# Attention and feed-forward in one hand-scheduled kernel: the adds of two vector engines kept apart in the built order, a cap on one engine's exps, and a reordered start

## The chip, the cores and the metric

The kernel runs on one core of a Trainium2 chip. The core has a matrix engine (TensorE, "PE" in the profile, with "PEld" for its weight loads), a vector engine (VectorE, "DVE"), a scalar engine (ScalarE, "ACT"), GpSimd ("POOL"), and a queue engine that issues DMAs (SyncE, "SP"). The engines run their own instruction lists and wait for one another by semaphores. The metric is the device time of one execution in microseconds; less is better.

## The reference

One token sequence (2048 x 640) is normalised and fed to two branches, whose results are added to the input.

```python
xn = _layernorm(x)                       # no scale, no bias
# A: attention, 32 query heads of 20, one shared key and value head
q = (xn @ wq) as [1, 32, 2048, 20];  k = xn @ wk;  v = xn @ wv
p = softmax(q k^T * 20 ** -0.5)
A = (p v, heads side by side) @ wo
# B: dense feed-forward of width 1728
B = silu(xn @ w1) @ w2
return x + A + B
```

Inputs and output are bfloat16.

## The kernel before

**How the work is tiled.** Scores are made transposed: a block is 128 keys of one head by 512 queries. There are 4 chunks of 512 queries, and in each 8 groups of 4 heads: 32 groups. A group has 16 key tiles (kt) times 4 heads (j) = 64 blocks, in the order kt, then j. Three blocks in a row are one step: `do_S` issues three score matmuls at once (each head lies in its own 32 rows), so there are 683 steps. Their three PSUM banks alternate between two sets of three.

**Two ways to make exp.** ScalarE turns two blocks of a step into exp with one ACTIVATE of 1024 columns (L841), or three with one of 1536. The third block usually goes to VectorE. `want_dve` decides: not in the first 8 steps, not in the last, not for the last two blocks of a group, and only if VectorE's planned backlog is under a threshold. VectorE's exp is an approximation by bits: L856 clips the score to a 16-bit integer (Z), which read as bfloat16 is a rough exponential. Two shifted copies of Z (Y) make it finer: the block's contribution is the sum of Z, Z+43 and Z+86, each multiplied with its own scaled copy of v. So a VectorE block gives three PV items and a ScalarE block one.

**The shifted adds.** `flush_z` collects up to three Z blocks and makes their two Y tiles: the second always on GpSimd (L888, int32 on pairs), the first on VectorE (L882) or GpSimd, by planned backlog.

**PV.** A round of `do_pv` takes up to one item from each of the four heads and multiplies them side by side in the four column strips of the array (L762). All rounds of a group add into one PSUM bank, U. When a group's items are done, VectorE copies U out (L931), a DMA transposes it, GpSimd divides (L920), and only then may the next group's rounds start. A head with more items than the others makes rounds in which fewer than four strips work. Exps of ScalarE wait for their round in a ring of 31 blocks (E).

**The rest of TensorE's work** is put in between the steps: query projections (`qd_job`, L977, spread to the heads by DMA), the hidden layer of the feed-forward (`h_job`, L1013, with a tanh on ScalarE at L1026 and a product on VectorE at L1031), and output rows (`out_job`, L1081 and L1086). `fill_chunk` gives each such job an earliest step, spread by PACE over the chunk. Where TensorE would stand idle and has recently been little used, `fill` adds matmuls on zeros (L684, L671), which keep its clock up.

**The order.** Nothing of the order is written out. `Sched` is a list scheduler that runs in Python when the kernel is built. Every operation has a planned duration and a priority (a smaller number first); each engine takes the ready operation with the least. TensorE's choice is `step`: S as soon as its banks are free, else a PV round or a job if it ends early enough before the next S is due (S_LEAD, OVER), else a fill. The lists are then fixed, and only true data dependences become semaphore waits. So planned times shape the order, but they do not hold an engine back on the chip.

**The lock.** `Op.lock` is part of that planning. An operation with the flag may not start, in planned time, before the last flagged operation of the other of VectorE and GpSimd has ended:

```python
if op.lock:
    r = max(r, self.lock_end["pool" if op.eng == "dve" else "dve"])
```

The VectorE adds carry it, and so do the norms, the division and the copies of k on GpSimd. GpSimd's adds (yp) do not.

**The prologue.** The input is loaded in 16 tiles, its statistics are taken on VectorE and ScalarE, the tiles are normalised on three engines and transposed, four to six on TensorE (L1453) and ten by DMA (L1421). `self.pro` is a queue of TensorE jobs, taken strictly from its head: four transposes, the first query tile (q0), k0, k1 and then the jobs of PRO. q0 and q1 (L952) give the queries of heads 0 to 3 and 4 to 7, each k job keys for two key tiles, each v job values for four. q1 needs its weights copied by ScalarE (L1316, priority 6; exps have 5). Step 21 is the first that reads q1. The zeros that the fills multiply are set by GpSimd (L1281).

Of the kernel before, what the change touches and what calls it, by code (L numbers as in the profile page):

```python
# [48 lines left out]
LATE_G = 0  # L49
AHEAD = 30  # L50
Q_FROM = 8
H0_STEP = 14
Y_SLOW = 0.1
H_FIRST = 4
NEARLY = 2
LASTPV = 16
DVE_LAST = 1
ZWAIT = 6
SWITCH = 0.105
S_LEAD = 0.56  # L60
PV_PRESS = 8
DVE_TH = 3.4
U_PRIO = 1.1
X_PRIO = 0.8
PACE = (0.9, 0.9, 0.9, 0.9)
WIN = 3.4
FILL_BELOW = 0.78
FILL_EARLY = 0.95
FILL_STEPS = 64
OVER = 0.1  # L70
PV_HOLD = 29
Q_EVERY = 2
DT_ISSUE = 1.28
UT_ISSUE = 1.05
DT = (4, 5, 6, 9, 10, 11, 12, 13, 14, 15)
NORM_P = 4.5
DVE_FROM = 8
NODB = 2
GB = 4 * KT
NB = NUNITS * KT  # L80
Y0_POOL = 1.0
Y0_COST = 1.45
YP_FIX = 0.14
YP_BLK = 0.47
PV_MIN = 4
PV_GO = 5
PRO = "v0 t7 t8 v1 k2 k3 k4 k5 v2 k6 k7 v3 q1 d0"
ACT_STATS = (4, 6, 9, 12, 14)
NW_ENG = ("dve", "dve", "dve")
NORM_ENG = ("pool", "pool", "pool", "pool", "act", "pool", "act", "act", "dve", "act", "act", "act")  # L90
# [254 lines left out]


def t_mm(n):
    return max(n, 64) / 2400.0 + 0.003


class Job:
# [15 lines left out]
class Builder:  # L367
# [88 lines left out]
    def steps_init(self):  # L456
        self.NG = NUNITS // 4
        self.T = -(-NB // 3)
        self.s_next = 0
        self.misc = deque()  # L460
        self.pro = deque()
        self.urgent = deque()
        self.cur_job = None
        self.pe_mode = None
        self.blk_pos = 0
        self.zset = 0
        self.zblocks = []
        self.exp_op = {}
        self.dve_steps = 0
        self.y0_pool = 0  # L470
        self.started = False
        self.pv_started = False
        self.tq = [[[] for _ in range(4)] for _ in range(self.NG)]
        self.begun = [False] * 4
        self.cg = 0
        self.g_seen = [0] * self.NG
        self.g_late = [0] * self.NG
        self.e_used = 0
        self.u_open = False
        self.u_last = []  # L480
        self.nfill = 0
        self.nqd = 0
        self.heldb = {}
        self.y_done = {}
        self.f_done = defaultdict(int)
        self.oT_made = set()
        self.pro_left = True
        self.filled = set()
        self.norm_made = defaultdict(int)
        self.first_step = {c: c * GB * 8 // 3 for c in range(QC)}  # L490
        self.first_step[QC] = self.T
# [80 lines left out]
    def step(self, now):  # L572
        sc = self.sc
        t = self.s_next
        sr = INF
        if t < self.T:
            sr = self.s_ready(t)
            if sr <= now + 1e-9:
                self.do_S(t, now)
                return True  # L580
        limit = INF
        if sr < INF:
            limit = sr
            e1 = self.exp_op.get(t - 1)
            if e1 is not None:
                endp = e1.end if e1.end is not None else sc.t["act"] + e1.dur
                limit = max(sr, endp - S_LEAD)
        pv_n, pv_some, pv_r = self.pv_ready(now)
        job = self.cur_job
        cand = None  # L590
        job_r = INF
        if job is None:
            for q in (self.urgent, self.pro, self.misc):
                if q:
                    r = self.job_ready(q[0])
                    if r <= now + 1e-9:
                        cand = q
                        break
                    job_r = min(job_r, r)
        has_misc = job is not None or cand is not None  # L600
        press = self.e_used > NBLK - PV_PRESS
        choice = None
        if pv_n and (self.pe_mode == "PV" or press):
            choice = "PV"
        elif has_misc and self.pe_mode == "M":
            choice = "M"
        elif pv_n >= PV_GO:
            choice = "PV"
        elif has_misc:
            choice = "M"  # L610
        elif pv_n:
            choice = "PV"
        nxt = min(sr, pv_r, job_r)
        if choice is None and pv_some >= (1 if press else PV_MIN):
            choice = "PV"
        if self.s_next >= self.T - LASTPV and (pv_n or self.s_next >= self.T and pv_some):
            choice = "PV"
        if choice is None:
            return self.fill(now, min(nxt, limit)) or nxt
        if choice == "PV":  # L620
            d = 0.216 + self.switch("PV")
        else:
            d = (job if job is not None else cand[0]).mms[0][0] + self.switch("M")
        if sr < INF and now + d > limit + OVER:
            return self.fill(now, limit) or (nxt if nxt > now else sr)
        if choice == "PV":
            self.do_pv(now, d)
        else:
            if job is None:
                job = cand.popleft()  # L630
                job.bank = self.bank_for_job(job)[1]
                self.cur_job = job
                if job.hold is not None:
                    self.heldb[job.hold] = job.bank
            self.do_mm(job, now, d)
        return True
# [10 lines left out]
    def fill(self, now, until):  # L647
        if self.s_next >= self.T and self.cg >= self.NG:
            return None
        sc = self.sc  # L650
        job = self.cur_job
        onto = job is not None and job.begun and job.width > 0 and (self.pe_mode == "M" or not self.u_open)
        mode = "PV" if self.u_open and not onto else "M"
        room = min(until, now + 0.33) - now - self.switch(mode)
        if room < 0.08 or self.busy_share(now) > (FILL_BELOW if self.s_next > FILL_STEPS else FILL_EARLY):
            return None
        n = min(512, int(room * 2400) // 32 * 32)
        after = ()
        if onto:
            n = min(n, job.width)  # L660
            b = job.bank
            ukey = ("B", b)

            def fn(pe):
                return pe.matmul(self.bk(b, 0, n), self.zero[:, 0:P], self.zero[:, 0:n], start=False, stop=False,
                                 skip_group_check=True)
        elif self.u_open:
            ukey = None

            def fn(pe):  # L670
                return pe.matmul(self.bk(UBANK, 0, n, 0, 32), self.zero[:, 0:32], self.zero[:, 0:n], start=False,  # L671
                                 stop=False, tile_position=(0, 0), skip_group_check=True)
        else:
            r, b = self.bank_for_job()
            ukey = ("B", b)
            if self.cur_job is not None or r > now + 1e-9:
                if not self.pv_started or self.u_open or not self.u_last:
                    return None
                if any(d.avail is None or d.avail > now for d in self.u_last):
                    return None  # L680
                b, ukey, after = UBANK, None, self.u_last

            def fn(pe):
                return pe.matmul(self.bk(b, 0, n), self.zero[:, 0:P], self.zero[:, 0:n], start=True, stop=True)  # L684
        z = sc.lastw.get(("zero",))
        if z is None or z.avail is None or z.avail > now:
            return None
        op = sc.new("pe", n / 2400.0 + self.switch(mode), fn, [("zero",)], [ukey] if ukey else [],
                    name="fill", queue=False)
        op.work = n / 2400.0  # L690
        op.deps.update(after)
        self.nfill += 1
        self.pe_mode = mode
        sc.commit(op, now)
        return True
# [51 lines left out]
    def do_pv(self, now, d):  # L747
# [24 lines left out]
            op.deps.add(sc.lastw[("vv", it.kt // 2)])  # L772
            self.e_used -= it.na
        op.mm = len(items)
        op.work = 0.216
        self.pe_mode = "PV"
        sc.commit(op, now)
        for it in items:
# [15 lines left out]

    def want_dve(self, t):
        g, kt, j = self.blocks(t)[-1]
        if t < DVE_FROM or 4 * kt + j >= GB - NODB or t >= self.T - DVE_LAST:
            return False
        sc = self.sc
        back = sc.t["dve"] - sc.t["pe"]  # L800
# [5 lines left out]
    def do_S(self, t, now):  # L806
# [42 lines left out]
        if dv:  # L849
            self.dve_steps += 1  # L850
            g, kt, j = bs[-1]
            zs, zp = self.zset, len(self.zblocks)
            bb = par3 + nh - 1

# [12 lines left out]
    def flush_z(self):  # L867
# [11 lines left out]
        for k, e in ((0, y0), (1, "pool")):  # L879
            yk = [("Y", zs, k, i) for i in range(n)]  # L880
            if e == "dve":
# [5 lines left out]
            cb = bass.AP(self.cy, c.offset, [list(c.ap[0]), [0, w // 2]])  # L887
            sc.new("pool", tp, lambda v, k=k, cb=cb: v.tensor_tensor(  # L888
                self.Y[:, zs, k, 0:w].bitcast(I32), self.Z[:, zs, 0:w].bitcast(I32), cb, ALU.add), zk + [("cy",)], yk,
                prio=4.0, name=f"yp{k}")  # L890
        for i, (t, g, kt, j) in enumerate(self.zblocks):
            for k in range(2):
                self.item(g, j, kt, k + 1, lambda k=k, i=i: self.Y[:, zs, k, i * QW:(i + 1) * QW].bitcast(BF16),
# [327 lines left out]
    def prologue(self):  # L1221
# [52 lines left out]
        def pool(d, fn, r, w, prio=0.0):  # L1274
            return np_("pool", d, fn, r, w, prio=prio, name="pool")
# [2 lines left out]
                                            fill=1.0, base=0, pattern=[[-1, P]], channel_multiplier=1),  # L1278
             [("idf",)], [("idf",)])
        pool(0.2, lambda g: g.tensor_copy(self.idb[:, :], self.idf[:, :]), [("idf",)], [("idb",)])  # L1280
        pool(0.3, lambda g: g.memset(self.zero[:, :], 0.0), [], [("zero",)])  # L1281
        pool(0.1, lambda g: g.memset(self.eps[:, :], EPS), [], [("eps",)])
        for k in range(2):
            pool(0.1, lambda g, k=k: g.memset(self.cy[:, k:k + 1], PH[k + 1][0] * 65537), [], [("cy",)])
# [300 lines left out]
```

## Time and profile before

| what | value |
|---|---|
| median of 3 runs | 739.06 us (738.40 to 739.63) |
| the profiled execution | 740.91 us, of which its instructions span 738.9 |
| mean granted clock of TensorE | 0.992 |
| first and last exp of ScalarE | start at 18.0 and 719.6 us |
| 60 to 719 us, busy of 659 | PE 639.4, DVE 609.4, ACT 644.0, POOL 461.3 |
| 719 to 738.9 us, busy of 19.9 | PE 16.5, DVE 8.3, ACT 3.2, POOL 2.5 |
| clock of TensorE at half | 0 to 7.2, 34.5 to 41.3, 48.1 to 51.5 us, and the last 1.3 us |

Some groups that stand beside the ones that the prediction shows:

```profile
L823 PE MATMUL psall<-sbt 32*128 32x512 bf16 x2048 | 268.2, 386 | 15.9 <-DVE sbt L856 10.9 <-ACT sbt L841 2.5 <-DVE sbt L1480 0.5
L762 PE MATMUL psall<-sbt 128*32 128x512 bf16 x3354 | 263.8, 386 | 4.6 <-DVE sbt L931 2.3 <-DVE sbt L882 1.0 <-POOL sbt L888 0.8
L882 DVE TENSOR_SCALAR sbt<-sbt 128x1024 int16<-128x1024 int16 x8 | 7.6, 956 | 0.2
L888 POOL TENSOR_TENSOR sbt<-sbt 128x512 int32<-128x512 int32 x12 | 13.9, 1169 | 3.3 <-DVE sbt L856 3.3
```

A line of this view has the source line, the engine and operation, what it writes and reads, the shape and the count; then the time in which at least one of the group was running, and the mean length of one in ns; then the idle time of the engine just before them and what ended it. Instructions of one engine overlap in their first and last tenths of a microsecond, so a mean length is more than the pace at which they follow each other. A row in order of time begins with its start and its length in us, the length being that of all its instructions together where it ends with a count.

### The profile page before, as it was taken

The numbers are of one execution on the slowest core, as the hardware profiler recorded it, in microseconds if no ns is written. First come the engines' busy times: TensorE is split into PE (matmuls) and PEld (weight loads), VectorE is DVE, ScalarE is ACT, GpSimd is POOL, SyncE is SP. The second block draws the span as 40 slices with busy tenths as digits, with TensorE's granted clock in tenths as the row PEclk, the third lists the DMA queues.
The fourth block names the chain that finished last, engine by engine and source line by source line (L and its number), as shares of the span: only waits on it lengthen the run. The fifth ranks groups of instructions, "written<-read, shape, count | busy, mean of one in ns | idle before, by whom it ended". The sixth has DMA issues, their size and how long they took to land.

```text
span 738.9 us, 17791 instructions
## 1 busy us (share of the span) xinstructions
PE 709.2 (96%) x6661; PEld 223.8 (30%) x6661; DVE 659.1 (89%) x1106; ACT 695.0 (94%) x775; POOL 489.8 (66%) x366
## 2 busy tenths in 40 slices
PE   9899999999999999999999999999999999999998
PEld 4422222233332322223333232222333223223334
DVE  6679989989998899999989899999998999999993
ACT  6979999999999999999999999999999999999990
POOL 3356766766777766767677676756775777566770
PEclk9979999999999999999999999999999999999999
DMA  9525310000010101000011011000001002000011
GB/s 283 113 84 154 110 15 19 12 16 16 9 45 9 43 25 34 20 19 8 8 11 43 8 59 37 16 16 16 8 2 43 10 8 62 27 8 1 9 37 36
DMA packets 52554, 27.69 MB, mean 37 GB/s; under 512 B 38422, under 2 KB 51830, under 8 KB 52470
## 3 DMA queue, kind: packets, MB, share of 16 engines
q1 hardware_dynamic: 51014, 26.35, 13.3%
q8 instruction: 54, 0.88, 0.5%
q10 hardware_dynamic: 1456, 0.22, 0.2%
q14 instruction: 30, 0.25, 0.1%
HBM read 11.44 MB, written 2.62 MB: 19 GB/s over the span
## 4 chain that ended last, share of the span: by engine, by line
PE 58%; DVE 19%; issue 11%; POOL 8%; ACT 3%; DMA 0%; POOLq 0%; DVEq 0%
PE psall L823 19%; PE psall L762 18%; DVE sbt L856 11%; PE psall L1081 9%; POOL sbt L888 8%; PE psall L1013 5%; DVE sbt L882 5%; PE psall L977 2%; PE psall L684 2%; PE psall L1086 1%; ACT sbt L841 1%; DVE sbt L1031 1%; ACT sbt L1362 1%; DVE sbt L931 1%; DVE sbt L1116 1%
## 5 line engine op out<-in xcount | busy, mean ns | idle before, releaser
L841 ACT ACTIVATE sbt<-psall 128x1024 bf16<-128x1024 f32 (+1 forms) x683 | 658.1, 1071 | 19.7 <-PE psall L823 16.3
L888 POOL TENSOR_TENSOR sbt<-sbt 128x768 int32<-128x768 int32 (+1 forms) x292 | 446.6, 1546 | 202.2 <-DVE sbt L856 158.6
L856 DVE TENSOR_SCALAR sbt<-psall 128x512 int16<-128x512 f32 x653 | 433.2, 682 | 49.0 <-PE psall L823 41.5
L823 PE MATMUL psall<-sbt 32*128 32x512 bf16 x2048 | 268.2, 386 | 15.9 <-DVE sbt L856 10.9
L762 PE MATMUL psall<-sbt 128*32 128x512 bf16 x3354 | 263.8, 386 | 4.6 <-DVE sbt L931 2.3
L823 PEld LDWEIGHTS psall<-sbt 32*128 32x128 bf16 x2048 | 68.2, 91 | 255.6 <-issue 98.0
L882 DVE TENSOR_SCALAR sbt<-sbt 128x1536 int16<-128x1536 int16 (+1 forms) x150 | 131.5, 876 | 2.7
L762 PEld LDWEIGHTS psall<-sbt 128*32 128x32 bf16 x3354 | 65.0, 94 | 119.4 <-issue 76.0
L1081 PE MATMUL psall<-sbt 128*128 128x320 bf16 x448 | 88.6, 303 | 0.0
L1013 PE MATMUL psall<-sbt 128*128 128x512 bf16 x260 | 79.2, 384 | 1.6 <-DVE sbt L1031 0.4
L1081 PEld LDWEIGHTS psall<-sbt 128*128 128x128 bf16 x448 | 34.3, 97 | 45.2 <-issue 33.1
L1031 DVE SCALAR_TENSOR_TENSOR sbt<-sbt,psall 128x512 bf16<-128x512 bf16 x54 | 36.6, 677 | 2.4 <-PE psall L823 1.1
L1026 ACT ACTIVATE sbt<-psall 128x512 bf16<-128x512 f32 x54 | 33.9, 628 | 0.2 <-DVE sbt L882 0.2
L977 PE MATMUL psall<-sbt 128*128 128x512 bf16 (+1 forms) x95 | 28.9, 385 | 0.6 <-DVE sbt L1031 0.6
L1086 PE MATMUL psall<-sbt 128*128 128x320 bf16 x144 | 29.1, 303 | 0.3 <-DVE sbt L1116 0.3
L920 POOL TENSOR_TENSOR sbt<-sbt 128x320 bf16<-128x320 bf16 x31 | 26.8, 865 | 3.8 <-DVE sbt L915 3.4
L1013 PEld LDWEIGHTS psall<-sbt 128*128 128x128 bf16 x260 | 17.1, 97 | 37.0 <-issue 22.2
L931 DVE CAST sbt<-psall 128x512 bf16<-128x512 f32 x32 | 21.8, 680 | 2.1 <-PE psall L762 2.1
L684 PE MATMUL psall<-sbt 128*128 128x512 bf16 (+2 forms) x76 | 20.3, 420 | 1.5 <-POOL sbt L1281 1.5
L1482 POOL TENSOR_SCALAR sbt<-sbt 128x256 bf16<-128x256 bf16 x8 | 4.1, 514 | 23.4 <-DVE sbt L1480 23.3
L1098 DVE SCALAR_TENSOR_TENSOR sbt<-psall,sbt 128x320 bf16<-128x320 f32 x28 | 13.5, 484 | 4.6 <-PE psall L1081 4.2
L1116 DVE SCALAR_TENSOR_TENSOR sbt<-psall,sbt 128x320 bf16<-128x320 f32 x28 | 13.2, 480 | 3.1 <-PE psall L1086 3.1
(81 smaller groups left out, 160.9 us busy)
## 6 DMA issues: line engine op xcount, KB each, us to landing
sbt<-in_A_x_dram SPq DMA_DIRECT2D x32, 160.0 KB, 3.4
out_dram<-sbt SPq DMA_DIRECT2D x15, 160.0 KB, 1.8
sbt<-in_B_w_dram SPq DMA_DIRECT2D x5, 432.0 KB, 6.3
sbt<-sbt SPq DMA_DIRECT2D x105, 20.0 KB
sbt<-in_B_w_dram SPq DMA_DIRECT2D x13, 160.0 KB, 3.0
sbt<-sbt SPq DMA_DIRECT2D x1, 1024.0 KB, 6.0
sbt<-sbt SPq DMA_TRANSPOSE x57, 2.4
sbt<-in_A_wo_dram SPq DMA_DIRECT2D x5, 160.0 KB, 2.7
```

Of the source, the lines that this page charges most:

```text
L684: return pe.matmul(self.bk(b, 0, n), self.zero[:, 0:P], self.zero[:, 0:n], start=True, stop=True)
L762: ins = pe.matmul(self.bk(UBANK, 0, QW, r, r + SLOT), self.v[:, it.w, it.kt, :], it.x(), start=f, stop=False, tile_position=(0, r), skip_g ...
L823: ins = pe.matmul(self.bk(par3 + i), self.kT[r:r + SLOT, kk, kt * P:(kt + 1) * P], self.qT[r:r + SLOT, g % 8, (g // 8) % 2, :], start=True ...
L841: return a.activation(self.E[:, b0 * QW:(b0 + na) * QW], self.ps[:, par3 * BANK:(par3 + na) * BANK], AF.Exp, scale=ACT_SCALE)
L856: return v.tensor_scalar(self.Z[:, zs, zp * QW:(zp + 1) * QW], self.bk(bb), 0.0, ZMAX, ALU.max, ALU.min)
L882: sc.new("dve", td, lambda v, k=k: v.tensor_scalar(self.Y[:, zs, k, 0:w], self.Z[:, zs, 0:w], float(PH[k + 1][0]), None, ALU.add), zk, yk, ...
L888: sc.new("pool", tp, lambda v, k=k, cb=cb: v.tensor_tensor(self.Y[:, zs, k, 0:w].bitcast(I32), self.Z[:, zs, 0:w].bitcast(I32), cb, ALU.ad ...
L977: return pe.matmul(self.bk(b, 0, QW, 0, rows), self.wq[:, k, lo:hi], self.xnT[:, k, c * QW:(c + 1) * QW], start=(k == 0), stop=(k == DC - 1))
L1013: return pe.matmul(self.bk(b), self.w1[:, k, fk * P:(fk + 1) * P], self.xnT[:, k, c * QW:(c + 1) * QW], start=(k == 0), stop=(k == DC - 1))
L1031: sc.new("dve", t_dve_ps(QW), lambda v: v.scalar_tensor_tensor(out=self.hT[0:rows, fk, :], in0=t, scalar=1.0, in1=src, op0=ALU.add, op1=AL ...
L1081: return pe.matmul(self.bk(b, 0, 320), self.hT[r0:r1, fk, i * P:(i + 1) * P], self.w2[r0:r1, fk, e0:e0 + 320], start=(m == 0), stop=(m == ...
L1086: return pe.matmul(self.bk(b, 0, 320), self.oT[:, k, i * P:(i + 1) * P], self.wo[:, k, e0:e0 + 320], start=(m == 0 and src != "ps"), stop= ...
```

## The change

It has five parts.

1. GpSimd's adds carry the lock flag, so that the planner keeps them and VectorE's flagged operations apart in planned time. The planned costs of both kinds of add are changed, and a partly filled set of Z blocks may wait 8 steps, not 6.
2. `want_dve` refuses a block if its head has had five VectorE blocks in its group. The threshold on the backlog is raised.
3. In the prologue q1 comes before k4 instead of after the last v job.
4. Fills planned before 5.6 us count at twice their length, since the clock is low there, and the zeros they use are set by VectorE.
5. Figures of the planner are changed: costs of a matmul and of a PV round, lead before a step, priorities, pace of the chunks, the priority of the norms. PV_MIN goes from 4 to 6.

```diff
-H0_STEP = 14
-Y_SLOW = 0.1
+H0_STEP = 13
+Y_SLOW = 0.085
-ZWAIT = 6
+ZWAIT = 8
-S_LEAD = 0.56
+S_LEAD = 0.616
-DVE_TH = 3.4
-U_PRIO = 1.1
-X_PRIO = 0.8
-PACE = (0.9, 0.9, 0.9, 0.9)
+DVE_TH = 4.25
+U_PRIO = 1.045
+X_PRIO = 0.88
+PACE = (0.9, 0.85, 1.1, 0.9)
-OVER = 0.1
+COLD = 5.6
+TILE_CAP = 5
+OVER = 0.125
-NORM_P = 4.5
+NORM_P = 2.5
-YP_FIX = 0.14
-YP_BLK = 0.47
-PV_MIN = 4
+YP_FIX = 0.185
+YP_BLK = 0.426
+PV_MIN = 6
-PRO = "v0 t7 t8 v1 k2 k3 k4 k5 v2 k6 k7 v3 q1 d0"
+PRO = "v0 t7 t8 v1 k2 k3 q1 k4 k5 v2 k6 k7 v3 d0"
...
 def t_mm(n):
-    return max(n, 64) / 2400.0 + 0.003
+    return max(n, 64) / 2400.0 + (0.008 if n > 400 else 0.006 if n > 300 else 0.003)
...
+        self.nz = [[0] * 4 for _ in range(self.NG)]
...
-            d = 0.216 + self.switch("PV")
+            d = 0.2215 + self.switch("PV")
...
-        room = min(until, now + 0.33) - now - self.switch(mode)
+        room = (min(until, now + (0.66 if now < COLD else 0.33)) - now - self.switch(mode)) / (2.0 if now < COLD else 1.0)
...
-        op = sc.new("pe", n / 2400.0 + self.switch(mode), fn, [("zero",)], [ukey] if ukey else [],
-                    name="fill", queue=False)
+        op = sc.new("pe", n / 2400.0 * (2.0 if now < COLD else 1.0) + self.switch(mode), fn, [("zero",)],
+                    [ukey] if ukey else [], name="fill", queue=False)
...
-        op.work = 0.216
+        op.work = 0.2215
...
-        if t < DVE_FROM or 4 * kt + j >= GB - NODB or t >= self.T - DVE_LAST:
+        if t < DVE_FROM or 4 * kt + j >= GB - NODB or t >= self.T - DVE_LAST or self.nz[g][j] >= TILE_CAP:
             return False
...
             g, kt, j = bs[-1]
+            self.nz[g][j] += 1
...
-                prio=4.0, name=f"yp{k}")
+                prio=4.0, name=f"yp{k}").lock = True
...
-        pool(0.3, lambda g: g.memset(self.zero[:, :], 0.0), [], [("zero",)])
+        np_("dve", 0.3, lambda v: v.memset(self.zero[:, :], 0.0), [], [("zero",)], prio=-1.0, name="zero")
```

## The prediction

> **What bounds the kernel now.** I read the page's busy times first, then the groups by shape, the waits, the stretches of time, and last the instructions in order of time around the places where ScalarE stands still.
>
> ```profile
> PE 709.2 (96%) x6661; PEld 223.8 (30%) x6661; DVE 659.1 (89%) x1106; ACT 695.0 (94%) x775; POOL 489.8 (66%) x366
> 100.00:150.00 50.00, 49.09 (x451) 13.44 (x448) 46.97 (x76) 49.97 (x59) 35.44 (x24) 1.00 0.09 19
> 250.00:300.00 50.00, 47.02 (x446) 13.96 (x449) 47.23 (x78) 47.14 (x53) 35.52 (x25) 1.00 0.15 41
> ```
>
> The first line is the page's, the two others are stretches (PE, PEld, DVE, ACT, POOL busy, granted clock, DMA). Three engines are near full, so no single one is the answer. In some stretches ScalarE never stops (49.97 of 50); in others it loses 2 to 3 us in 50. The metric is therefore ScalarE: how long its work is when it never waits, plus what it waits.
>
> ```profile
> L841 ACT ACTIVATE sbt<-psall 128x1024 bf16<-128x1024 f32 x654 | 620.9, 1053 | 19.0 <-PE psall L823 15.9 <-ACT sbt L841 0.4
> L841 ACT ACTIVATE sbt<-psall 128x1536 bf16<-128x1536 f32 x29 | 42.0, 1466 | 0.6 <-PE psall L823 0.5
> L856 DVE TENSOR_SCALAR sbt<-psall 128x512 int16<-128x512 f32 x653 | 433.2, 682 | 49.0 <-PE psall L823 41.5 <-POOL sbt L888 0.9
> L882 DVE TENSOR_SCALAR sbt<-sbt 128x1536 int16<-128x1536 int16 x142 | 123.8, 872 | 2.5
> L888 POOL TENSOR_TENSOR sbt<-sbt 128x768 int32<-128x768 int32 x280 | 432.9, 1563 | 198.9 <-DVE sbt L856 155.3 <-PE psall L823 26.4 <-issue 4.1
> ```
>
> Neighbouring exps overlap: "mean 1053 ns" is not their pace. From the list of ScalarE instructions in order of time, back-to-back two-block exps start 0.903 us apart (the shortest, and the 25th percentile; the median is 0.91), three-block ones 1.330, a tanh takes 0.476. Adding up what each interval has above these, from the first exp (18.0 us) to the last (719.6), gives 38.3 us of lost ScalarE time in 174 places. So of about 702 us between them 664 are ScalarE's floor.
>
> I sorted those places by what the late step's score matmul S had just waited for. In 51 places (16.3 us) S began within 0.25 us of the end of VectorE's exp of two steps before, which frees its bank: VectorE was late. In 123 (21.5 us) TensorE was still at other work or behind; one (0.2 us) was another. The largest place, and one in the prologue, look alike:
>
> ```profile
> 556.41 2.89 POOL L888 TENSOR_TENSOR sbt<-sbt 128x768 int32<-128x768 int32 x2
> 558.02 1.69 DVE L882 TENSOR_SCALAR sbt<-sbt 128x1536 int16<-128x1536 int16 x1
> ...
> 560.04 1.95 DVE L856 TENSOR_SCALAR sbt<-psall 128x512 int16<-128x512 f32 x3
> 560.86 0.39 PE L823 MATMUL psall<-sbt 32*128 32x512 bf16 x3 [0.99 <-DVE sbt L856]
> 561.18 0.40 PE L762 MATMUL psall<-sbt 128*32 128x512 bf16 x4
> 561.29 1.94 ACT L841 ACTIVATE sbt<-psall 128x1024 bf16<-128x1024 f32 x2 [1.54 <-PE psall L823]
> ```
>
> The shifted add on VectorE (L882) lies beside two of GpSimd's (L888), takes 1.69 us instead of 0.55 and holds up the VectorE exp behind it; S waits, ScalarE stands 1.54 us.
>
> **The change, part by part.** The profiled execution spans 738.9 us (740.9 with what lies around the span; the runs' median is 739.06). I sum on the span and apply the difference to the median.
>
> *Shifted adds apart.* Only L882 had looked at the other engine's lock; now the yp on GpSimd takes and respects it too. No semaphore is added: only the built order moves. An L882 without any GpSimd work beside it takes 0.548 us; the 142 average 0.872 and the eight smaller 0.956 against 0.426. That is 142 x 0.324 + 8 x 0.53 = 50 us of VectorE time inside contention. GpSimd's 1.563 against 1.464 alone is 28 us on an engine with a third of its time free. If half of VectorE's 50 us go, it becomes about 25 us less busy and, what counts, its exps stop being late. Best end: all 16.3 us of VectorE-caused loss, plus a little of the lateness that it passes to TensorE: -19. Other end: the adds now queue for a gap, behind them are the PV matmuls of their blocks, and at the end of each of 32 groups TensorE's U bank waits for the last; a tenth of a GpSimd add (0.146 us) uncovered per group is 4.7: +5. What covers it is the ring of 31 exp blocks, some 15 steps. I take -8.5, half of the 16.3 (half the contention), nearer the best end because the place above shows the whole path from add to ScalarE.
>
> [...] I hold that the exps of VectorE, which read PSUM and take 0.68 with or without GpSimd beside them, can run meanwhile.
>
> *At most five.* Steps have three of a group's 64 blocks; the last goes to VectorE. By the rules in the code 30 of 683 steps may not: 653 remain, and there are 653 L856, so the threshold never refused and raising it does nothing. Counting indices, 21 groups (numbers 1 or 2 modulo 3) have 21 such blocks, six on one head; the sixth goes to ScalarE now. So 21 exps grow from 0.903 to 1.330: +9.0 us of ScalarE. VectorE loses 21 L856 (601 ns pace): -12.6 us. Each VectorE block gives three PV items instead of one, and the head with six sets a group's rounds: 28 become 26. Start times show 873 rounds now, 34 of one matmul alone; 42 fewer at 0.218 are -9.2 us of TensorE. Matmuls on L762 go from 3354 to 3312. Ends: wholly on ScalarE's path, +9; wholly relieving TensorE, -7 after what its min-step pacing gives away. In the stretches where ScalarE never stops (100 to 250, 300 to 450 and 500 to 550, more than half) it costs, elsewhere it helps: 0.55 x 9.0 - 0.45 x 0.7 x 9.2 = +2.
>
> *The start.* COLD halves the number of fill matmuls planned below 5.6 us.
>
> ```profile
> 1.46 11.39 PE L684 MATMUL psall<-sbt 128*128 128x512 bf16 x39 [1.46 <-POOL sbt L1281]
> 9.55 1.50 DVE L1367 TENSOR_SCALAR sbt<-sbt 128x640 bf16<-128x640 bf16 x4
> 12.69 1.28 PE L1453 MATMUL psall<-sbt 128*128 128x128 bf16 x20
> 13.17 0.70 ACT L1461 ACTIVATE sbt<-psall 128x640 bf16<-128x640 bf16 x1 [2.96 <-PE psall L1453]
> ```
>
> The first normalised tile is there at about 10.0, the first transpose starts at 12.69: fills stand before it, 0.43 us each until about 7.3 and 0.21 after (the clock record has half speed to 7.2). The 36 before the first transpose count 36 x 0.216 = 7.8 us in the plan and took 11. Removing some ten at 0.21 to 0.43 lets it start at about 10.4; the last of four tiles is normalised at 11.05, so the gain is at most 2.6. Taken -2.0; 0 if the later transposes by DMA rule anyway. Zeroing on VectorE costs nothing: it stands idle until 3.14 us (uncovered, 0.53 by GpSimd's row).
>
> [...]
>
> *Second q tile.* q1 (five matmuls at L952, one VectorE evacuation, no DMA; it is moved past k4 to k7 and three v, whose evacuations and GpSimd copies move behind it) ran at 49.8, and step 21, the first that reads it, started ScalarE 0.87 late. Steps 19 to 21 lost 2.15: best end -2.2. It now waits for its weight copy on ScalarE (L1316, 0.53 us, at 43.6, below exps in priority), with k4 queued behind and step 10's S for that: at worst 0.53 + 5 x 0.2 = +1.5. Taken -1.0.
>
> *The rest* (lead, pace, priorities, cost figures) issues the same instructions in another order: -3 to +3; the nearest rows are 70 losses of 20 to 100 ns that more lead can close, taken -0.5. PV_MIN does nothing: it asks for more tiles than four exist, or for four when all are ready. NORM_P only moves ten norms ahead; its cover is the DMA transposes.
>
> Sum: -8.5 + 2.0 - 2.0 - 1.0 - 0.5 = -10.0. On the span 728.9, on the median **729**.
>
> **Rivals.**
> *A, ScalarE takes its price (slower).* The three-block exps fall where ScalarE never stops and VectorE's relief goes nowhere since TensorE is late there: +9.0 - 2.0 (start) = **746**. For it: 49.97 of 50. Against it: 38 us are lost somewhere. It decides once less than 7 us of those 38 are won back.
> *B, the order doesn't hold on the chip.* Nothing but planned time keeps the adds apart; real ones drift and L882 stays above 0.8. Then -2 - 1 + 2 - 0.5 = -1.5: **737.6**. For it: L1293 to L1302 on GpSimd take 0.19 where 0.15 is planned. Against: an add's planned cost is now 1.46, which is what it takes alone.
> *C, all of it.* VectorE stops being late and TensorE's relief reaches its 21.5 us too: -19 - 3 + 2 = **719**.
>
> **Numbers.** Forecast 0.54, A 0.19, B 0.17, C 0.10. About 0.2% (1.5 us) is what a measurement tells from no change: 737.6 to 740.5. B splits 0.08 faster, 0.06 within, 0.03 slower; so faster 0.72, same 0.06, slower 0.22. The forecast's own range is 723 to 736; over all, 718 to 745 leaves out most of A's worse half and C's best end.
>
> **What would show it.** L856 x632, exps of 1536 x50, L762 x3312 are sure. L882 near 0.6 shows the lock holding; near 0.8 is B. ScalarE's losses above pace should fall from 38 to about 25; near 38, with the time above 740, is A. The first exp should start near 16 us, q1 before 40. I am wrong if adds stay short and ScalarE still waits, for then the lost time had another source.

## The result, and the profile after

The changed kernel takes 716.96 us (median; 715.75 to 718.75) against 739.06. The ratio is 0.9703, 95% interval 0.9676 to 0.9731: 22 us faster, where 10 were forecast. Its profiled execution spans 716.2 us of 718.16.

The page's line of busy times, and the two stretches that were shown of before:

```profile
PE 693.8 (97%) x6592; PEld 219.0 (31%) x6592; DVE 614.3 (86%) x1059; ACT 695.8 (97%) x775; POOL 498.4 (70%) x392
```
```profile
100.00:150.00 50.00, 48.05 (x451) 13.38 (x455) 45.15 (x73) 49.59 (x57) 36.06 (x27) 1.00 0.06 15
250.00:300.00 50.00, 49.12 (x466) 14.06 (x466) 43.98 (x75) 49.70 (x56) 37.62 (x29) 1.00 0.13 35
```

ScalarE is at work 49.6 us or more of 50 in both, and 49.4 or more in every 50 us from 100 to 700, where 47.1 was the least before. VectorE has 45 us less work, GpSimd 9 more. The groups by shape:

```profile
L844 ACT ACTIVATE sbt<-psall 128x1024 bf16<-128x1024 f32 x633 | 600.5, 1108 | 3.8 <-PE psall L826 3.0
L892 POOL TENSOR_TENSOR sbt<-sbt 128x768 int32<-128x768 int32 x288 | 431.9, 1517 | 169.8 <-DVE sbt L860 129.3 <-PE psall L826 21.4 <-PE psall L765 8.7
L860 DVE TENSOR_SCALAR sbt<-psall 128x512 int16<-128x512 f32 x632 | 427.5, 687 | 74.8 <-PE psall L826 66.4 <-POOL sbt L892 1.1
L886 DVE TENSOR_SCALAR sbt<-sbt 128x1536 int16<-128x1536 int16 x114 | 81.3, 714 | 0.7
L844 ACT ACTIVATE sbt<-psall 128x1536 bf16<-128x1536 f32 x50 | 73.3, 1506 | 0.9 <-PE psall L826 0.8
```

The counts are those forecast: 632 VectorE exps, 50 wide ScalarE exps. VectorE's adds (L882 before, L886 now) average 0.714 us, not 0.872, and there are 114, not 142: 21 blocks fewer need them, and the planner sends more of the rest to GpSimd. ScalarE's idle time before a two-block exp is 3.8 us, from 19.0. The mean exp is longer, 1.108 and not 1.053, but its pace is not: from one two-block exp to the next 0.903 us is the shortest in both traces, and the median is 0.904, from 0.911. So more of each record lies beside its neighbour's; why it does is not shown.

The start, in order of time:

```profile
1.19 8.23 PE L687 MATMUL psall<-sbt 128*128 128x512 bf16 x30 [1.19 <-DVE sbt L1285]
9.42 1.50 DVE L1371 TENSOR_SCALAR sbt<-sbt 128x640 bf16<-128x640 bf16 x4
10.00 1.44 PE L1457 MATMUL psall<-sbt 128*128 128x128 bf16 x20 [0.58 <-DVE sbt L1371]
10.47 0.70 ACT L1465 ACTIVATE sbt<-psall 128x640 bf16<-128x640 bf16 x1 [0.46 <-PE psall L1457]
```

TensorE now waits for the normalised tile, and no longer the tile for the fills.

I did the same sum as in the prediction for both traces: first exp; ScalarE's floor (0.903, 1.330 and 0.476 us an instruction, the few others at their own length) to the last exp; every lateness of 20 ns or more over it, by what the step's S had waited for; and the tail, from the start of the last exp to the end. Lateness under 20 ns, 2 to 3 us in all, stands nowhere.

| us | before | after | difference |
|---|---|---|---|
| start to first exp | 18.0 | 15.4 | -2.6 |
| floor | 660.7 | 669.6 | +8.9 |
| lost behind VectorE's exp | 16.3 | 3.6 | -12.7 |
| lost behind TensorE and others | 22.0 | 11.8 | -10.2 |
| tail | 19.3 | 13.5 | -5.8 |

So the price of the cap was paid in full, and the four other rows gave back 31 us. One of them, the tail, is in no term of the prediction.

### The profile page after: what moved, and what is told of

Same layout as the page of the kernel before. It is cut to its first block, busy times and chain, and to the rows that moved or that the text cites. A ratio compares the mean times of both kernels' runs of the same rounds, so it can differ in the third digit from the quotient of the medians.

```text
span 716.2 us, 17658 instructions
## 1 busy us (share of the span) xinstructions
PE 693.8 (97%) x6592; PEld 219.0 (31%) x6592; DVE 614.3 (86%) x1059; ACT 695.8 (97%) x775; POOL 498.4 (70%) x392
## 4 chain that ended last, share of the span: by engine, by line
PE 60%; ACT 25%; DVE 7%; issue 6%; DMA 1%; DVEq 0%; ACTq 0%; SPq 0%; POOL 0%; POOLq 0%
ACT sbt L844 22%; PE psall L826 21%; PE psall L765 18%; PE psall L1085 8%; PE psall L1017 6%; PE psall L981 3%; ACT sbt L1030 2%; DVE sbt L886 2%; DVE sbt L860 2%; PE psall L1090 2%; DVE sbt L1035 1%; DVE sbt L1346 1%; PE psall L687 1%; ACT sbt L1366 1%; DMA sbt<-sbt 1%
## 5 line engine op out<-in xcount | busy, mean ns | idle before, releaser
L892 POOL TENSOR_TENSOR sbt<-sbt 128x768 int32<-128x768 int32 (+2 forms) x319 | 458.4, 1456 | 176.3 <-DVE sbt L860 135.8
L860 DVE TENSOR_SCALAR sbt<-psall 128x512 int16<-128x512 f32 x632 | 427.5, 687 | 74.8 <-PE psall L826 66.4
L765 PE MATMUL psall<-sbt 128*32 128x512 bf16 x3312 | 250.4, 385 | 3.8 <-DVE sbt L935 2.1
L765 PEld LDWEIGHTS psall<-sbt 128*32 128x32 bf16 x3312 | 60.9, 95 | 108.2 <-issue 71.1
L1085 PE MATMUL psall<-sbt 128*128 128x320 bf16 x448 | 89.7, 303 | 0.0
L886 DVE TENSOR_SCALAR sbt<-sbt 128x1536 int16<-128x1536 int16 (+2 forms) x123 | 88.6, 723 | 0.8
L1085 PEld LDWEIGHTS psall<-sbt 128*128 128x128 bf16 x448 | 33.5, 97 | 47.3 <-issue 35.6
L1030 ACT ACTIVATE sbt<-psall 128x512 bf16<-128x512 f32 x54 | 38.0, 704 | 0.0
L1017 PEld LDWEIGHTS psall<-sbt 128*128 128x128 bf16 x260 | 17.1, 97 | 37.0 <-issue 22.8
L935 DVE CAST sbt<-psall 128x512 bf16<-128x512 f32 x32 | 21.9, 683 | 2.7 <-PE psall L765 2.5
L687 PE MATMUL psall<-sbt 128*128 128x512 bf16 (+5 forms) x57 | 16.2, 442 | 1.5 <-DVE sbt L1285 1.2
L1120 DVE SCALAR_TENSOR_TENSOR sbt<-psall,sbt 128x320 bf16<-128x320 f32 x28 | 13.3, 483 | 3.5 <-PE psall L1090 3.4
L1090 PEld LDWEIGHTS psall<-sbt 128*128 128x128 bf16 x144 | 10.9, 97 | 14.2 <-issue 7.8
```

Source lines behind the costliest of these rows:

```text
L765: ins = pe.matmul(self.bk(UBANK, 0, QW, r, r + SLOT), self.v[:, it.w, it.kt, :], it.x(), start=f, stop=False, tile_position=(0, r), skip_g ...
L860: return v.tensor_scalar(self.Z[:, zs, zp * QW:(zp + 1) * QW], self.bk(bb), 0.0, ZMAX, ALU.max, ALU.min)
L886: sc.new("dve", td, lambda v, k=k: v.tensor_scalar(self.Y[:, zs, k, 0:w], self.Z[:, zs, 0:w], float(PH[k + 1][0]), None, ALU.add), zk, yk, ...
L892: sc.new("pool", tp, lambda v, k=k, cb=cb: v.tensor_tensor(self.Y[:, zs, k, 0:w].bitcast(I32), self.Z[:, zs, 0:w].bitcast(I32), cb, ALU.ad ...
L1017: return pe.matmul(self.bk(b), self.w1[:, k, fk * P:(fk + 1) * P], self.xnT[:, k, c * QW:(c + 1) * QW], start=(k == 0), stop=(k == DC - 1))
L1030: sc.new("act", t_act(QW), lambda a: a.activation(t, src, AF.Tanh, scale=0.5), [("B", b)], [("tb", tp)], prio=X_PRIO, name=f"th{c}_{fk}")
```

## The experiments

L, T, N, C, P and Q in the expectations are the theories explained there; C stands for another one in each group of runs. Each kernel is timed beside the kernel before, and the ratios are to it. Kernels whose name begins with a are the changed one with something taken back; those with b are the one before with something put in. In the tables, "lost" is the lateness over the floor, with VectorE's part of it in brackets.

**One part taken back.** Four kernels.

```diff
# a_nolock
-                prio=4.0, name=f"yp{k}").lock = True
+                prio=4.0, name=f"yp{k}")
# a_nocap
-TILE_CAP = 5
+TILE_CAP = 16
# a_oldstart: the old PRO, NORM_P, H0_STEP, zeros by GpSimd, and
-COLD = 5.6
+COLD = 0.0
# a_oldnum: the old ZWAIT, S_LEAD, DVE_TH, U_PRIO, X_PRIO, PACE, OVER,
# PV_MIN, YP_FIX, YP_BLK, Y_SLOW, t_mm, and the old cost of a PV round
```

> The changed kernel with the lock flag of GpSimd's adds taken off again. Theory L (the flag wins back most of the 22.9 us of ScalarE loss, through VectorE): VectorE's 1536-wide adds go back from 0.71 to about 0.85 us, ScalarE's loss from 15 to 25 or more, time 727 to 733. Theory T (the cap's relief of TensorE did it: 43 fewer rounds): time 717 to 720, loss under 19, whatever the adds do. Theory N (the planner's corrected figures did it): as T.

> The changed kernel with no cap (16 allowed). 653 VectorE exps and some 873 rounds again; ScalarE's floor falls by 8.9 to about 661. Theory L: loss stays near 15 and the tail after the last exp near 13.5, so 708 to 716, faster than the changed kernel. Theory T: the loss goes back to 30 or more and the tail from 13.5 to 19, so 722 to 735.

> The changed kernel with the old start: q1 last, fills not counted double, zeros by GpSimd, norms and first feed-forward step as before. All theories: first exp back at 18.0 from 15.4; time 719.5 to 723. If the start did more than its 2.6 us, for instance by setting the loss of the first 100 us (8.6 before, 3.6 after), up to 725.

> The changed kernel with the planner's old figures (costs of adds, matmul and round, lead, over, priorities, pace, threshold). Theory N: loss back to 25 or more, 727 to 735. Theories L and T: 717 to 721, loss 15 to 19.

| kernel | us | ratio (95%) | first exp | floor | lost (VectorE) | tail |
|---|---|---|---|---|---|---|
| a_nolock | 738.52 | 0.9989 (0.9972 to 1.0006) | 15.5 | 669.6 | 30.7 (15.0) | 16.7 |
| a_nocap | 735.03 | 0.9942 (0.9924 to 0.9960) | 15.5 | 659.2 | 21.8 (11.1) | 33.8 |
| a_oldstart | 731.31 | 0.9893 (0.9875 to 0.9910) | 17.4 | 669.6 | 25.0 (7.3) | 14.7 |
| a_oldnum | 737.83 | 0.9977 (0.9964 to 0.9990) | 16.0 | 669.8 | 34.9 (9.4) | 11.7 |

Each costs 14 to 22 us, together 75, out of a gain of 22. Three of the times lie above the ranges given, a_nocap at the end of its own. Without the flag the adds are back at 0.854 us and the loss behind VectorE at 15.0: that is theory L, only larger than it said.

```profile
L886 DVE TENSOR_SCALAR sbt<-sbt 128x1536 int16<-128x1536 int16 x113 | 96.5, 854 | 2.1
```

Without the cap the floor falls by 10.4 us (8.9 by the exps, the rest because three tanh run after the last exp); the loss rises by 6.4 us, and VectorE's part of it by 7.5; the tail grows by 20 us. Stretches of the tail, only the matmuls of the feed-forward's half of the output rows (L1081 before, L1085 in the two others; start:end, length, PE busy, PEld busy), of before, after and a_nocap:

```profile
719.63:738.90 19.27, 7.03 (x42) 3.84 (x42) 0.97 0.10 35
```
```profile
702.69:716.20 13.51, 0.93 (x3) 0.28 (x3) 1.00 0.14 50
```
```profile
698.88:732.70 33.82, 16.96 (x112) 10.26 (x112) 1.00 0.06 20
```

After the last exp 42 such matmuls were left before, 3 are now, and 112 in the changed kernel without its cap. So without the cap TensorE carries unfinished work past the steps. The 43 rounds more (873 against 830) are 9.4 us of it at 0.218 each; the last exp also comes 3.8 us sooner, and between the first and the last exp TensorE stands idle 25.9 us there and 16.6 in the changed kernel. Why it idles more is not shown.

**Is it this one order?** Every edit makes the planner lay out the whole kernel anew. So the changed kernel was built twice with a planner figure moved by 1%.

```diff
# a_switch99
-SWITCH = 0.105
+SWITCH = 0.10395
# a_y0cost101
-Y0_COST = 1.45
+Y0_COST = 1.4645
```

> The changed kernel with one planner figure moved by 1% (SWITCH 0.105 to 0.104): another order, the same edits. Theory P (the changed kernel's order is a lucky one among many that the same edits give, and taking any edit out falls back to the usual): 725 to 738, with loss 25 or more. Theory C (the edits work together and each is needed): 717 to 722, loss 14 to 19, since all of them are in.

> A second re-drawn order of the changed kernel: Y0_COST 1.45 to 1.4645. Theory P: 725 to 738. Theory C: 717 to 723, loss 14 to 19, tail within 4 us of the changed kernel's 13.5.

720.58 us (0.9731, 0.9705 to 0.9757; lost 17.4, tail 13.3) and 722.42 us (0.9767, 0.9740 to 0.9794; lost 16.7, tail 16.1). Theory C holds: with all edits in, the three orders give 717 to 722. Some 5 us between kernels of this family are chance of the order, and no single difference that small between two orders is read as a cause below. The changed kernel is the fastest of the three, so some 2 to 5 of its 22 us (by the ratios) may be a lucky draw. The kernel before was built in one order only; how far another draw of it would lie was not tried.

**One part put in.**

```diff
# b_lock: the flag, and the new YP_FIX, YP_BLK, Y_SLOW
+                prio=4.0, name=f"yp{k}").lock = True
# b_cap
+TILE_CAP = 5
# b_lockcap: both
# b_start: the new PRO, NORM_P, H0_STEP, COLD, zeros by VectorE
+PRO = "v0 t7 t8 v1 k2 k3 q1 k4 k5 v2 k6 k7 v3 d0"
```

> The kernel before with the lock flag on GpSimd's adds and the new costs of the adds, nothing else. Theory L of the prediction: VectorE's adds fall from 0.87 to about 0.7 us, VectorE-caused loss from 16 to under 8, time 727 to 732. Theory C (TensorE and VectorE must both be relieved): the adds are as short, but TensorE stays late, time 733 to 738.

> The kernel before with the cap of five alone. Floor 669.6, 830 rounds. By the prediction's net of +2: 739 to 743. Theory T (the cap's relief of TensorE is worth more than its price): tail from 19.3 to about 14, loss under 28, time 730 to 735. Rival A of the prediction: 746.

> The kernel before with lock and cap, old start and old planner figures. If the two add up (728.1 and 737.8 alone, against 739.5), 726. Theory C (the lock's loss and the cap's tail are different places, and only together are VectorE and TensorE both free): floor 669.6, loss 16 to 20, tail 12 to 14, 719 to 724.

> The kernel before with the new start alone (q1 ahead of k4, fills counted double below 5.6 us, zeros by VectorE, norms and the first feed-forward step earlier). By the prediction's terms -3.0: 735 to 737. Theory Q (q1's weight copy on ScalarE comes late here as in the run with the old figures, where it ran at 34.7 us and not at 25.3, and k4 stands behind q1): first exp at 15.5 to 16 but a loss of 6 to 9 more at steps 10 to 21, 738 to 746.

| kernel | us | ratio (95%) | first exp | floor | lost (VectorE) | tail |
|---|---|---|---|---|---|---|
| b_lock | 728.13 | 0.9837 (0.9814 to 0.9859) | 17.1 | 660.7 | 23.8 (8.5) | 21.9 |
| b_cap | 737.78 | 0.9968 (0.9953 to 0.9983) | 16.7 | 669.6 | 33.2 (17.6) | 12.1 |
| b_lockcap | 726.62 | 0.9829 (0.9809 to 0.9850) | 16.7 | 669.6 | 22.5 (5.4) | 12.4 |
| b_start | 746.86 | 1.0099 (1.0081 to 1.0116) | 15.2 | 660.8 | 46.1 (17.0) | 19.3 |

The lock alone, with its costs of the adds, gives 11.8 us, in the loss: 7.8 us less behind VectorE and 6.4 behind TensorE, against a tail that is 2.6 longer. Its group of VectorE's adds:

```profile
L882 DVE TENSOR_SCALAR sbt<-sbt 128x1536 int16<-128x1536 int16 x125 | 87.6, 702 | 1.0
```

0.702 us and not 0.872. The cap alone pays 8.9 in the floor and has 7.2 back in the tail and 5.1 in the loss, where TensorE's part falls by 6.2 and VectorE's rises by 1.3. Its time, 2.2 us less than the kernel before, lies between the two that were expected, and within the chance of the order. Lock and cap simply add up (theory C of that run misses). The new start alone is slower, just above what theory Q said, and it is one queue. ScalarE and TensorE's q1 in b_start, in order of time:

```profile
29.52 4.62 ACT L842 ACTIVATE sbt<-psall 128x1536 bf16<-128x1536 f32 x4
33.98 0.58 ACT L1317 ACTIVATE sbt<-sbt 128x400 bf16<-128x400 bf16 x1
34.62 1.25 PE L953 MATMUL psall<-sbt 128*128 128x512 bf16 x5
38.14 2.86 ACT L842 ACTIVATE sbt<-psall 128x1024 bf16<-128x1024 f32 x3 [3.58 <-PE psall L824]
...
50.61 1.94 ACT L842 ACTIVATE sbt<-psall 128x1024 bf16<-128x1024 f32 x2 [4.91 <-PE psall L824]
```

and in the changed kernel:

```profile
25.30 0.54 ACT L1320 ACTIVATE sbt<-sbt 128x400 bf16<-128x400 bf16 x1
...
28.18 1.24 PE L956 MATMUL psall<-sbt 128*128 128x512 bf16 x5
```

The copy of q1's weights (L1317, L1320) has a priority behind that of the exps. In b_start it runs at 34.0, after the last exp that was ready; q1 waits for it, k4 to k7 wait behind q1 in the queue that is taken from its head, and ScalarE stands still 3.6 us at step 10 and 4.9 at step 16. In the changed kernel it runs at 25.3.

**The late copy.** What sends it early there? One cost in the plan would do, and a priority should.

```diff
# a_tmm
-    return max(n, 64) / 2400.0 + (0.008 if n > 400 else 0.006 if n > 300 else 0.003)
+    return max(n, 64) / 2400.0 + 0.003
# b_startwq = b_start, a_tmmwq = a_tmm, a_oldnumwq = a_oldnum, each with
-                [("wqd", kk)], [("wq", kk)], prio=1.0 + 5 * kk, name=f"wq{kk}")
+                [("wqd", kk)], [("wq", kk)], prio=1.0 + 2.5 * kk, name=f"wq{kk}")
# a_oldpro: the changed kernel with the old PRO alone
```

> The changed kernel with the old cost of a matmul alone (0.003 us of overhead and not 0.008 or 0.006). Theory Q: this one figure decides in the plan whether q1's weight copy comes before the exps; the copy is late, ScalarE loses 7 to 9 us more before 60 us, loss after 100 us stays near 12, time 725 to 732. If the old figures hurt by a worse fit all along, loss after 100 us is over 18.

> The run with the new start alone (746.9), with one more edit: q1's weight copy on ScalarE gets a priority ahead of the exps (3.5, not 6). Theory Q: the copy no longer runs at 34.0, the lumps at steps 10 to 18 (some 12 us) go, and what is left of the new start against the kernel before is its earlier first exp and q1 in time: 734 to 738. If the new start hurts in another way: 742 to 747.

> The changed kernel with the old cost of a matmul (733.7), and q1's weight copy ahead of the exps. Theory Q: the better cost of a matmul matters only by letting that copy go early: 717 to 723, loss before 100 us under 5. If the cost matters by itself: 726 to 733.

> The changed kernel with the old place of q1 alone (after the last v job); fills and zeros as changed. First exp at 15.4 to 15.6. If q1's place is what the new start brings in this kernel, step 21 waits 3 to 4 us for q1 and the order after it is another: 725 to 731, near the run with the whole old start (731.3) less its 2 us. If the fills are what matters: 717 to 720.

> The changed kernel with all the planner's old figures (737.8) and q1's weight copy ahead of the exps. If the old figures hurt only by the late copy: 719 to 724, as with the old matmul cost alone (721.1). If lead, round cost and costs of the adds are worth something of their own: 725 to 731, with the loss after 100 us above 15 and VectorE's adds above 0.74.

| kernel | us | ratio (95%) | lost in the first 100 us | lost later | tail |
|---|---|---|---|---|---|
| a_tmm | 733.71 | 0.9917 (0.9894 to 0.9939) | 13.3 | 18.0 | 12.5 |
| a_tmmwq | 721.12 | 0.9744 (0.9723 to 0.9765) | 8.0 | 11.3 | 13.9 |
| b_startwq | 736.09 | 0.9938 (0.9917 to 0.9959) | 7.5 | 29.4 | 19.2 |
| a_oldnumwq | 731.00 | 0.9878 (0.9852 to 0.9905) | 4.6 | 24.6 | 11.7 |
| a_oldpro | 728.49 | 0.9842 (0.9826 to 0.9858) | 4.4 | 18.8 | 14.9 |

The copy in a_tmm, a_tmmwq and b_startwq, and ScalarE's step 21 in a_oldpro:

```profile
34.23 0.58 ACT L1320 ACTIVATE sbt<-sbt 128x400 bf16<-128x400 bf16 x1
```
```profile
19.56 0.53 ACT L1320 ACTIVATE sbt<-sbt 128x400 bf16<-128x400 bf16 x1
```
```profile
20.05 0.53 ACT L1317 ACTIVATE sbt<-sbt 128x400 bf16<-128x400 bf16 x1
```
```profile
49.16 1.02 ACT L844 ACTIVATE sbt<-psall 128x1024 bf16<-128x1024 f32 x1 [3.41 <-PE psall L826]
```

Theory Q is shown for the start: an early copy takes 10.8 us off the new start alone and 12.6 off the kernel with the old matmul cost, and what steps 10 to 18 lose falls from 12 to 3 us in the one and from 11 to 3 in the other. Five nanoseconds of planned cost decided when the copy ran. Not all of the 12.6 is the start: a_tmm is slower than its range and loses 18.0 us after 100 us, where near 12 was expected, and a_tmmwq 11.3. Those 6.7 us come with the order after the start, and nothing here says why. (In a_tmmwq the first 100 us lose 8.0, more than the 5 expected; 3.9 of them are at steps 52 and 53, long after the copy.)

The rest of the old figures keep 14 us even with the copy early (731.0 against 717.0; 9.9 against a_tmmwq, which differs in them alone), mostly lost later than 100 us and with adds at 0.753 us. Which of them does it was not tried apart. With q1 in its old place step 21 waits 3.4 us for it, but the first 100 us lose only 0.8 more than in the changed kernel; 7.1 of that kernel's 11.5 us are lost later and 1.4 in the tail.

**Order or length.** Two ways to make the lock real, as semaphores.

```diff
# a_hard (on the changed kernel) and b_lockhard (on b_lock), in commit
         if op.lock:
             self.lock_end[e] = op.end
+            other = self.lock_op["pool" if e == "dve" else "dve"]
+            if other is not None:
+                op.deps.add(other)
+            self.lock_op[e] = op
# b_tie, on the kernel before, whose plan lets the adds overlap
+        if op.name in ("y0", "y1", "yp0", "yp1"):
+            other = self.add_op["pool" if e == "dve" else "dve"]
+            if other is not None:
+                op.deps.add(other)
+            self.add_op[e] = op
```

> The changed kernel, its planned order kept, with the lock made real: each flagged operation also waits by semaphore for the last one of the other engine that was planned before it. Every 1536-wide add of VectorE takes 0.55 to 0.57. If time inside contention is what costs, the 18 us in it go and the 3.6 us of VectorE-caused loss shrink: 712 to 715. If a wait before the add is as long as one within it, and only the order counts: 716 to 719.

> The kernel before, its order unchanged, with each shifted add waiting by semaphore for the last add of the other engine that was planned before it. No add lies beside another: VectorE's 1536-wide ones take 0.55 to 0.57 and not 0.87. If only the order counts (the wait moves from within the add to before it): 736 to 742, loss 35 to 40. If length inside contention were the cost by itself: 727 to 733, as with the lock in the plan.

> The kernel before with the lock in the plan (728.1) and the same lock as semaphores. If semaphores help wherever the plan already keeps the adds apart (as in the changed kernel, -3): 723 to 727, adds at 0.56, VectorE-caused loss under 6. If they pass lateness from engine to engine (as in the kernel before, +36): 730 to 740.

The semaphores leave the built order as it is: VectorE, ScalarE and GpSimd run the same instructions in the same order as in the kernel that each was made from. So the chance of the order plays no part here. a_hard takes 713.84 us (0.9653, 0.9637 to 0.9669), faster than both kernels; lost 11.3, of which 0.4 behind VectorE. b_lockhard takes 720.97 (0.9743, 0.9722 to 0.9765); lost 15.7, 7 us better than b_lock and below its range. b_tie takes 775.63 (1.0480, 1.0463 to 1.0497), slower than either of its two expectations. VectorE's adds in a_hard and in b_tie:

```profile
L891 DVE TENSOR_SCALAR sbt<-sbt 128x1536 int16<-128x1536 int16 x114 | 63.3, 556 | 16.0 <-POOL sbt L897 14.0
```
```profile
L888 DVE TENSOR_SCALAR sbt<-sbt 128x1536 int16<-128x1536 int16 x142 | 85.8, 605 | 68.6 <-POOL sbt L894 66.5
```

Short adds are not the point. In b_tie they take 0.605 us (18 of the 142 lie beside other GpSimd work, which is not tied there), and VectorE waits 68.6 us in front of them: 154 in all, where the kernel before spent 126 on them (124 in the adds, 2.5 in front). The loss behind VectorE goes from 16.3 to 40.6. In a_hard the two make 79 us, hardly less than the changed kernel's 82. The order is planned without overlap in a_hard and with it in b_tie; that, and not the length of an add, tells the two results apart. (b_tie also ties fewer operations, the adds alone; tying more did no harm in b_lockhard.) One add and the wait in front of it come to 0.89 us before, 0.71 in b_lock, 0.70 in a_hard, 0.64 in b_lockhard and 1.09 in b_tie, and the loss behind VectorE to 16.3, 8.5, 0.4, 3.6 and 40.6. That the semaphores help by holding each engine to its plan is my reading of it, not shown.

## Why the prediction was right in kind and wrong in size

**Shifted adds apart: -8.5; measured -11.8 alone.** The mechanism is shown, from the add to ScalarE, by a_nolock, b_lock and the loss by cause. The half that I took of the 16.3 us behind VectorE is what came (7.8). The size was off because the term as taken holds none of the 21.5 us behind TensorE: in b_lock they fell by 6.4, with nothing done for TensorE. That part looks like knock-on as well; it is little more than the chance of the order. The adds stopped between my two signs, at 0.702 and 0.714 us, so the plan holds on the chip only in part; a_hard shows that the rest was worth 3 us.

**At most five: +2; measured -2.2 alone, which is within the chance of the order, and 18.1 lost when taken out.** The floor rose by the 8.9 foreseen. The failing step is the weighting that let TensorE's 9.2 us count only where ScalarE waits, 2.9 us in all. In b_cap TensorE's part of the loss fell by 6.2, and the tail, which stands in no term, by 7.2: TensorE's unfinished jobs wait at the end of the list, and 42 feed-forward output matmuls of the kernel before ran after the last exp. Rival A had the right price and missed the same payback.

**The start: -2.0; measured -2.6**, of which the kernel before explains a part itself: with its start unchanged, b_lock, b_cap and b_lockcap had their first exp at 16.7 to 17.1. The clock tells these runs apart. With the old start the first exp comes at 16.7 where full clock comes at 4.4 or 4.5 us (b_lockcap, b_cap) and at 18.0 where it comes at 7.2 (before); with the new one at 15.4 for 4.6 (the changed kernel) and 15.8 for 7.1 (b_startwq). So by these four the new start is worth 1.3 us with an early clock and 2.2 with a late one; the term was about right, and the 2.6 is partly luck of the profiled execution.

**Second q tile: -1.0, at worst +1.5; measured, together with the fills, +7.0 on the kernel before (b_start), and -4.0 with the copy early (b_startwq).** The queue that I named is what happened. The bound was wrong: I priced one step's wait, but k5 to k7 stood behind the same queue, and steps 13, 16 and 18 paid again. In the changed kernel the copy ran at 25.3, so the term did no harm there; that hung on 5 ns of a planned cost, which I did not foresee. It is luck.

**The rest: -0.5; wrong.** "The same instructions in another order" is a change of its own here: 14 us between 731.0 and 717.0. I sized it by the 70 smallest losses; what came was spread over the run, and which figure brings it stays open.

**The sum** took the parts as separate terms. They are not: taken out one at a time they cost 75 us. Adding them from the front, lock and cap give 13.2 where I had 6.5, and the last 9.7 come only with start and figures together, for which I had 3.5; the miss of 12 us is about half in each. Start without figures is a_oldnum (737.8; it hits the late copy, and with the copy early still takes 731.0; it also has the old costs of the adds), figures without start is a_oldstart (731.3).

Rival B fell: the flag does shorten the adds on the chip, to below its 0.8. Rival C (719) was nearest, for a reason that is half its own: TensorE's lateness did fall, by 10.2 of its 22 us, but another 5.8 came in the tail, which it does not name, and the order drawn was a good one.

## What to carry to other kernels

Split a pipelined kernel's time as start, floor of the busiest engine, its lateness by cause, and tail, and give every edit an entry in each of the four; work saved on a second engine that is always behind can appear after the last step (7.2 us here). Where a planner in Python sets the order, a planned cost is an edit like any other: rebuild with a figure moved by 1% to learn how much is chance (here 5 us) before a small difference is explained. Keep engines apart in the plan first; here semaphores that enforce it helped only then (3 and 7 us, against 36 lost).

## What the runs showed of the hardware

In the kernel before, VectorE's shifted add of 1536 columns took 0.548 us where no GpSimd work lay beside it (3 of 142), and up to 1.76 beside GpSimd's; GpSimd's of 768 took 1.464 with none of VectorE's adds beside it (108 of 280), and up to 1.85. The 53 VectorE adds that began while no GpSimd instruction ran took 0.56 us at most, also when one began beside them (49 of the 53); the 97 others averaged 1.05. Of GpSimd's 280 adds of 768 the 80 that began while one of VectorE's ran averaged 1.80, the other 200 averaged 1.47. So of two adds that met there, the one that started later was the long one on average. VectorE's exps took 0.682 us on average: 0.683 for the 333 that lay wholly beside GpSimd work, 0.681 for the 171 with none beside them. Kept apart in the plan, VectorE's adds took 0.702 us in b_lock, and its time was 0.9837 of that of the kernel before.

TensorE's full clock came at 7.2 us in the profile of the kernel before, and at 3.8 to 6.0 in those of a_hard, b_start, the changed kernel (4.6) and a_nocap, with the first fill at 1.5 in the kernel before and at 1.2 in these. So from the first fill it took 2.6 to 5.7 us in these five. In the kernel before the fills up to then mostly started 0.427 us apart, and those after it 0.216. Later dips to half speed last 3.4 us or 6.8 (34.5 to 41.3 and 48.1 to 51.5 us in the kernel before, 18.2 to 21.6 and 35.3 to 38.7 in the changed one). In the 3.41 us ahead of these four TensorE was busy 2.32, 2.20, 1.99 and 2.52 us, in the last 3.41 of each dip all the time. What decides on a dip is not shown: TensorE was busy 2.42 us of the 3.41 from 557.45 us in the kernel before, and no dip followed. Nor is it shown how much of the clock the fills keep up, since every kernel here has them. The profiled execution of before was at the late end, and part of its 18.0 us to the first exp is that: with the same start and full clock at 4.4 or 4.5 the first exp came at 16.7 (b_lockcap, b_cap).
